# Linear attention and a mixture of adapters on one core: numerators one slot ahead, q three slots ahead, gating a step later

## The chip, the cores and the metric

The kernel runs on one core of one Trainium2 chip. The metric is the device time of one execution in microseconds (us). The engines are TensorE (PE, with the loads of its weights as PEld), VectorE (DVE), ScalarE (ACT), GpSimd (POOL) and SyncE (SP). Each has its own queue and they meet through semaphores. L257 is line 257 of the kernel before.

## The reference

Inputs are q, k and v of 8 batches, 8 heads, 576 positions and 64 features in fp32, and the weights of 8 adapters of rank 16. Cut to what matters:

```python
def phi(x):                     # c, s: cos and sin of pi/2 * position / 576
    r = np.maximum(x, 0.0)
    return np.concatenate([r * c, r * s], axis=-1)
q_p, k_p = phi(q), phi(k)                            # 128 features
kv = np.einsum('bhsf,bhsd->bhfd', k_p, v)            # per batch and head
z = np.sum(k_p, axis=2)
x = (q_p @ kv) / (q_p @ z + 1e-06)                   # heads side by side: 4608 x 512
logits = x @ w_gate                                  # 8 experts, the best two are taken
w = softmax over the two
out = x + sum over the two of w * ((x @ A[e]) @ B[e])
```

## The kernel before, in words

A batch has 576 = 9 x 64 positions; position 9 r + s is row r of block s. Two blocks make a *slot* of 128 tokens, so 8 batches make NT = 36 slots; slots 4, 13, 22 and 31 hold block 8 of two batches (`mixed`). The first slots that need kv of batch 1 to 7 are 4, 9, 13, 18, 22, 27 and 31.

The whole program order is written out by hand (`manual_schedule`): what a step emits stands in each engine's queue in just this order. The main loop runs over steps n = 0 to 34, and what the steps do is put together from these pieces:

- **k.** `load_k`, `load_q`, `load_v` are DMAs that POOL issues and that turn fp32 into bf16. A block of k is scaled by cos and by sin with its relu, as two instructions on ACT, on DVE (`scale_k1`, L151 and L153) or on POOL (L156); POOL's need the relu before them, `relu_k` on DVE (L165). `kv` (L180) multiplies a scaled block by v into the PSUM tiles `cd`; after the ninth block of a batch `kv_out` copies them on ACT (L188). The tables `kv_at`, `relu_at`, `pool_at`, `act_at` and `dve_at` say in which step each row stands; `first` is the batch's first slot, `at` the step in which its relus stand and its POOL rows start. When POOL's rows of batch b are issued, the loads of k and v of batch b + 3 and of q of batch b + 2 follow in its queue.
- **q.** `move_q(n)` turns the q of slot n with 16 (from slot 27 on 32 smaller) matmuls by diagonal matrices into two PSUM tiles of the pool `qd` (L213, L201), which has two buffers, and two copies with relu on ACT put it into `qpT` (L229).
- **Numerators.** `numden(n)` (L257) multiplies `qpT` by kv into `nd`, the 8 heads' numerators and denominators. `nd` has one buffer. Epsilon is added by a small matmul (L252), or, in steps after 13 that have rows of `kv`, by DVE (`eps_dve`).
- **Normalise.** `normalise(n)` on DVE: the reciprocal (L270) and the product (L277), giving `xt`, the slot's x.
- **Transposition.** `transp_x(n)` (L285) turns `xt` with four matmuls into the PSUM tile `xz`, of which there is one, and `evac_x` copies it on DVE (L291).
- **Logits and gate.** `logits(n)` (L311) gives gate logits and x A for all experts of a slot into `za` (one buffer for a group of three slots). Per group: `gate_a` on DVE (L320 to L328), `gate_sig` on ACT (L337), `gate_b` on DVE (L344, L346), then `transp_z` (L359) into the rest of `xz`, which the next `evac_x` takes along.
- **Output.** `emit(d)` is two matmuls, x by the identity and the gated part by B (L377, L382), a copy on ACT (L408) and the store by SP; later slots take the second matmul alone and add x on POOL (`delta_add`, L397, L402). In steps with rows of `kv` the output takes a buffer of `qd`, otherwise `cd`.

Step n stands in this order: `evac_x(n-1)`, `normalise(n)`, `move_q(n+1)`, rows of `kv`, early logits, gates, outputs, the sigmoid, `transp_x(n)`, `transp_z`, rows and relus of k, late logits, `numden(n+1)`, rows of k on ACT.

The stores are held back until k of the last batch has landed (`first_loads`). After the loop the last groups are gated and put out one by one.

Of the kernel before, what the change touches and what calls it, by code (L numbers as in the profile page):

```python
# [13 lines left out]
NS = 9  # L14
# [5 lines left out]
def kernel(ctx, tc, q, k, v, w_gate, A, Bw, out):  # L20
# [12 lines left out]

    persist = ctx.enter_context(tc.tile_pool(name="persist", bufs=1))
    p_kp = ctx.enter_context(tc.tile_pool(name="p_kp", bufs=3))
    p_qpt = ctx.enter_context(tc.tile_pool(name="p_qpt", bufs=6))
    p_kv = ctx.enter_context(tc.tile_pool(name="p_kv", bufs=3))
    p_x = ctx.enter_context(tc.tile_pool(name="p_x", bufs=14))
    p_xt = ctx.enter_context(tc.tile_pool(name="p_xt", bufs=7))
# [24 lines left out]
    def load_k(b, eng=None):  # L64
        load(eng or nc.gpsimd, k_b[b].rearrange("p g s d -> p g (s d)"), k, b)

    def load_q(b):
        load(nc.gpsimd, q_b[b].rearrange("p g s d -> p g (s d)"), q, b)

    def load_v(b):  # L70
        load(nc.gpsimd, v_b[b][:, 0:VN].rearrange("p (g x) -> p g x", g=G), v, b)
# [161 lines left out]
    def move_q(n):  # L233
        transp_q(n)
        evac_q(n, 0)
        evac_q(n, 1)
# [5 lines left out]
    def numden(n):  # L242
        nd_t[n] = nd = ps.tile([128, 2, 512], FP32, name="nd")
        tok = tokens(n)
        if mixed(n):
            jobs = [(lo, tok[0][0]), (hi, tok[1][0])]
        else:
            jobs = [(slice(0, 128), tok[0][0])]
        for gg in range(2):
            qpT = qpT_t.pop((n, gg))  # L250
            if not eps_dve(n):
                nc.tensor.matmul(out=nd[:, gg, D:4 * W:W], lhsT=ones, rhs=eps_hi, start=True,  # L252
                                 stop=False, skip_group_check=True)
            for j in range(4):
                h = 2 * j + gg if quad(n) else gg * 4 + j
                for pr, b in jobs:
                    nc.tensor.matmul(out=nd[pr, gg, j * W:(j + 1) * W],  # L257
                                     lhsT=qpT[:, j, pr], rhs=kv_t[b][:, h % 2, h // 2, :],
                                     start=(eps_dve(n) and j == 0), stop=(j == 3),
                                     skip_group_check=True)  # L260
# [21 lines left out]
    def transp_x(n):  # L282
        x = xt_t[n].rearrange("p (k c) -> p c k", c=DCH)
        for c in range(DCH):
            nc.tensor.transpose(out=xz[:, c * 128:(c + 1) * 128], in_=x[:, c], identity=ident)  # L285
# [140 lines left out]
    def put(at, step, what):  # L426
        at.setdefault(step, []).append(what)
# [5 lines left out]
    kv_at[3] = [(1, s) for s in (5, 4, 7, 8, 6)]  # L433
    for b in range(2, B):
        first = b // 2 * NS + b % 2 * 4
        at = {2: 5, 3: 8, 4: 12, 5: 17, 6: 20, 7: 23}[b]
        n_pool = {2: 5, 3: 7, 4: 8, 5: 8}.get(b, 9)
        for s0, s1 in ((0, 3), (3, n_pool)):
            put(relu_at, at, (b, s0, s1))
        for s in range(n_pool):  # L440
            put(pool_at, at, (b, s))
        for i in range(2):
            if n_pool <= 7:
                put(dve_at, at, (b, 7, i))
            if n_pool < 9:
                put(act_at, first - 4 + i, (b, 8, i))
            if n_pool == 5:
                put(act_at, first - 3 + i, (b, 6, i))
                put(act_at, first - 2, (b, 5, i))
        order = (7, 0, 1, 2, 3, 4, 8, 6, 5) if n_pool <= 7 else (0, 1, 2, 3, 4, 5, 8, 6, 7)  # L450
        if n_pool == 9:
            order = range(NS)
        for j, s in enumerate(order):

            if b == 2:
                ahead = 2 if j < 4 else 1
            elif b == 3:
                ahead = 3 if j < 2 else 2 if j < 5 else 1
            else:
                ahead = 4 - min(j // 2, 3)  # L460
            put(kv_at, first - ahead, (b, s))

    early_at, late_at, gate_a_at, gate_b_at, move_at = {}, {}, {}, {}, {}
    prev = 5
    for g, t in enumerate(groups[:-2]):
        at = max(t[-1] + 1, prev + 1)
        for n in t:
            if t[-1] + 1 < at or (n < t[-1] and prev == at - 1):  # L470
                put(late_at, at - 1, n)
            else:
                put(early_at, max(n + 1, at - 1), n)
        prev = at + 1
        put(gate_a_at, at, g)
        put(gate_b_at, at + 1, g)
        put(move_at, at + 2, g)
    put(late_at, NT - 2, NT - 3)

    with tc.manual_schedule():  # L480
# [17 lines left out]
        load_q(2)  # L498
        load_k(3)
        load_v(3)  # L500
        load_k(4)
        load_q(3)
        load_v(4)
        kv_out(0)
        transp_q(0)
        evac_q(0, 0, "dve")
        evac_q(0, 1)
        numden(0)

        g10, g11, g12 = range(len(groups) - 3, len(groups))  # L510
        todo, held = [], []
# [11 lines left out]
                held.append(d)  # L523

        for n in range(NT - 1):
            if n > 0:
                g = move_at.get(n - 1, (None,))[0]
                evac_x(n - 1, g)
                if g is not None:
                    todo += groups[g]  # L530
            normalise(n)
            if n != 3:
                move_q(n + 1)
            for b, s in kv_at.get(n, ()):
                kv(b, s)
                if kv_n[b] == NS:
                    kv_out(b)
            for t in early_at.get(n, ()):
                logits(t)
            if n == 3:  # L540
                move_q(n + 1)
            for g in gate_a_at.get(n, ()):
                gate_a(g)
            for g in gate_b_at.get(n, ()):
                gate_b(g)
            now = todo[:2 if len(todo) > 3 and n not in kv_at else 1]
            del todo[:len(now)]
            for d in now:
                emit(d, n not in kv_at, add=n > 27)
            for g in gate_a_at.get(n, ()):  # L550
                gate_sig(g)
            transp_x(n)
            for g in move_at.get(n, ()):
                transp_z(g)
            for b, s, i in dve_at.get(n, ()):
                scale_k1(b, s, i, "dve")
            for b, s0, s1 in relu_at.get(n, ()):
                relu_k(b, s0, s1)
            for b, s in pool_at.get(n, ()):
                scale_k(b, s)  # L560
                if (b, s) == pool_at[n][-1]:
                    if b + 3 < B:
                        load_k(b + 3)
                    if b + 2 < B:
                        load_q(b + 2)
                    if b + 3 < B:
                        load_v(b + 3)
                    if b + 3 == B - 1:

                        nc.sync.dma_start(out=first_loads, in_=k_b[B - 1][0:1, 0, 0, 0:8])  # L570
                        for d in held:
                            store(d)
                        held = None
            for t in late_at.get(n, ()):
                logits(t)
            numden(n + 1)
            for b, s, i in act_at.get(n, ()):
                scale_k1(b, s, i, "act")

# [56 lines left out]
```

## Time and profile before

| | before |
|---|---|
| time, median of 3 runs | 114.4 us (114.37 to 114.47) |
| the profiled execution: time | 114.54 us |
| its span | 112.8 us |
| PE busy, share of the span | 96.1 us, 85% |
| DVE | 83.7 us, 74% |
| ACT | 78.2 us, 69% |
| POOL | 72.3 us, 64% |

The profile is of one execution. "Busy" is the time in which an engine runs instructions; a group's row says how many instructions of one line there are, their busy time and mean, the engine's idle time just before them and what ended it. In a timeline a row gives the start, the length, the engine, the line and the tiles; equal neighbours are merged, and on PE the length reaches a little into the next row, since matmuls are pipelined.

### The profile page before, as it was taken

What the parts mean: (1) busy time and instruction counts of PE and PEld (TensorE: products, weight loads), DVE (VectorE), ACT (ScalarE), POOL (GpSimd) and SP (SyncE); (2) the same over time, 40 slices, a digit from 0 to 9 for tenths busy, and PEclk for the clock granted to TensorE, in tenths of its full rate; (3) what the DMA queues carried; (4) which work ended last, traced back from release to release, by engine and by line L of the source; (5) the groups of instructions that cost most, each with busy time, mean ns of one, the idle gap of its engine ahead of it and who ended that gap; (6) DMA issues with size and microseconds to landing.
All of it is one profiled execution on the core that took longest, in us unless ns stands there. A gap on an engine that the chain in (4) does not pass through costs nothing.

```text
span 112.8 us, 4956 instructions
## 1 busy us (share of the span) xinstructions
PE 96.1 (85%) x2050; PEld 74.1 (66%) x2068; DVE 83.7 (74%) x296; ACT 78.2 (69%) x169; POOL 72.3 (64%) x134
## 2 busy tenths in 40 slices
PE   2999676978899899999999999998998997978710
PEld 1347465867796788868788888785786886754200
DVE  5598489459969677695987998999949589786620
ACT  5087579755986595797876978856777777895720
POOL 5992223228995996299939999989980445774000
PEclk9999999999999999999999999999999999999998
DMA  2999999999999999999999999999999424526892
GB/s 41 385 206 208 213 202 210 210 180 208 208 208 209 207 209 209 209 206 213 204 207 208 208 209 208 242 348 383 381 324 366 142 100 97 185 101 226 285 340 82
DMA packets 19670, 24.77 MB, mean 220 GB/s; under 512 B 2624, under 2 KB 14528, under 8 KB 19648
## 3 DMA queue, kind: packets, MB, share of 16 engines
q0 software_dynamic: 13856, 13.84, 73.8%
q1 hardware_dynamic: 5792, 10.62, 26.9%
q8 instruction: 16, 0.26, 0.9%
q14 instruction: 6, 0.05, 0.1%
HBM read 28.85 MB, written 9.44 MB: 340 GB/s over the span
## 4 chain that ended last, share of the span: by engine, by line
PE 40%; DMA 28%; DVE 15%; issue 4%; POOL 4%; ACT 4%; POOLq 0%; DVEq 0%; ACTq 0%
DMA k<-in_k_dram 14%; DMA v<-in_v_dram 12%; PE cd L180 9%; PE za L311 7%; PE qd L213 6%; PE xz L285 5%; PE nd L257 4%; DVE xt L277 4%; PE dx L377 3%; DVE k L165 3%; DVE xT L291 2%; DVE zg L346 2%; ACT osb L408 2%; PE qd L201 2%; DMA out_dram<-osb 2%
## 5 line engine op out<-in xcount | busy, mean ns | idle before, releaser
L229 ACT ACTIVATE qpT<-qd 128x512 bf16<-128x512 f32 x71 | 38.6, 595 | 15.0 <-PE qd L213 10.9
L156 POOL TENSOR_SCALAR kp<-k,cos_tab 128x256 bf16<-128x256 bf16 x46 | 22.6, 490 | 7.1 <-DVE k L165 6.5
L277 DVE TENSOR_TENSOR xt<-nd,rden 128x512 bf16<-128x512 f32 x36 | 24.9, 691 | 1.3
L291 DVE COPY xT<-xz 128x512 bf16<-128x512 bf16 (+1 forms) x36 | 17.1, 476 | 9.9 <-PE xz L359 6.4
L156 POOL TENSOR_SCALAR kp<-k,sin_tab 128x256 bf16<-128x256 bf16 x46 | 21.9, 476 | 0.0
L180 PE MATMUL cd<-v,kp 64*128 64x128 bf16 x576 | 20.3, 217 | 0.9 <-DVE kp L153 0.9
L285 PEld LDWEIGHTS <-xt 128*128 128x128 bf16 x144 | 10.8, 115 | 12.1 <-DVE xt L277 7.9
L285 PE MATMUL xz<-ident,xt 128*128 128x128 bf16 x144 | 14.4, 222 | 5.0 <-DVE xt L277 4.3
L180 PEld LDWEIGHTS <-kp 64*128 64x128 bf16 x576 | 16.3, 94 | 3.1 <-issue 0.9
L257 PE MATMUL nd<-kvsb,qpT 128*128 128x65 bf16 (+1 forms) x320 | 16.7, 195 | 1.1 <-DVE qpT L231 0.5
L213 PE MATMUL qd<-diag,q 128*64 128x128 bf16 x432 | 17.3, 222 | 0.3 <-DMA q<-in_q_dram 0.3
L402 POOL TENSOR_TENSOR osb<-osb,xt 128x512 f32<-128x512 f32 x8 | 9.2, 1160 | 9.6 <-ACT osb L408 8.0
L408 ACT COPY osb<-dx 128x512 f32<-128x512 f32 x19 | 11.2, 588 | 5.9 <-remote 2.1
L213 PEld LDWEIGHTS <-q 128*64 128x64 bf16 x432 | 13.1, 109 | 1.8 <-DMA q<-in_q_dram 0.5
L257 PEld LDWEIGHTS <-qpT 128*128 128x128 bf16 (+1 forms) x320 | 12.7, 100 | 1.9 <-ACT qpT L229 0.7
L311 PE MATMUL za<-AW,xT 128*128 128x144 bf16 x140 | 12.4, 227 | 0.7 <-DVE zg L346 0.5
L311 PEld LDWEIGHTS <-xT 128*128 128x128 bf16 x144 | 9.0, 98 | 3.2 <-DVE xT L291 1.0
L408 ACT COPY osb<-cd 128x512 f32<-128x512 f32 x16 | 9.1, 597 | 1.3 <-PE cd L382 1.3
L62 POOL DMA_DIRECT2D v<-in_v_dram x8 | 6.2, 778 | 5.2 <-DMA q<-in_q_dram 4.4
L485 PE MATMUL wu<-wide,ones 128*128 128x512 bf16 x24 | 7.3, 477 | 2.0 <-DVE AW L115 2.0
L62 POOL DMA_DIRECT2D q<-in_q_dram x8 | 6.1, 763 | 3.6 <-DMA k<-in_k_dram 3.6
L62 POOL DMA_DIRECT2D k<-in_k_dram x7 | 5.4, 771 | 3.9 <-DMA k<-in_k_dram 2.2
(75 smaller groups left out, 133.8 us busy)
## 6 DMA issues: line engine op xcount, KB each, us to landing
out_dram<-osb SPq DMA_DIRECT2D x32, 256.0 KB, 3.9
v<-in_v_dram POOLq DMA_DIRECT2D x8, 576.0 KB, 16.5
q<-in_q_dram POOLq DMA_DIRECT2D x8, 576.0 KB, 15.6
k<-in_k_dram POOLq DMA_DIRECT2D x7, 576.0 KB, 15.5
k0f<-in_k_dram SPq DMA_DIRECT2D x1, 1152.0 KB, 5.4
out_dram<-osb SPq DMA_DIRECT2D x8, 128.0 KB, 2.4
AW<-in_moe_A_dram POOLq DMA_DIRECT2D x1, 128.0 KB, 18.2
Ball<-in_moe_B_dram POOLq DMA_DIRECT2D x1, 128.0 KB, 16.7
```

What stands on the lines that cost most here:

```text
L62: eng.dma_start(out=t, in_=rows(dram, b))
L156: nc.gpsimd.tensor_scalar(out=dst, in0=src, scalar1=tab, scalar2=1.0, op0=ALU.mult, op1=ALU.mult)
L180: nc.tensor.matmul(out=kvz[par][:, g], lhsT=kp_t[b][pr, s, g], rhs=v_rhs(b, g, s, pr), start=(first and g == 0), stop=(last and g == G - 1))
L213: nc.tensor.matmul(out=t[cols, j, 2 * gi:2 * gi + 2, :], lhsT=q_b[b][:, 2 * gp + gi, s, :], rhs=diag[:, s, i], start=(j == 0 and gi == 0), ...
L229: nc.scalar.activation(t, src, AF.Relu)
L257: nc.tensor.matmul(out=nd[pr, gg, j * W:(j + 1) * W], lhsT=qpT[:, j, pr], rhs=kv_t[b][:, h % 2, h // 2, :], start=(eps_dve(n) and j == 0), ...
L277: nc.vector.tensor_tensor(out=x, in0=nd[:, :, :, 0:D], in1=rden.rearrange("p (g j) -> p g j", g=2).to_broadcast([128, 2, 4, D]), op=ALU.mult)
L285: nc.tensor.transpose(out=xz[:, c * 128:(c + 1) * 128], in_=x[:, c], identity=ident)
L291: nc.vector.tensor_copy(t[:, 0:c], xz[:, 0:c * 128].rearrange("p (c s) -> p c s", c=c))
L311: nc.tensor.matmul(out=za_t[g][:, i, :], lhsT=xT[:, c, :], rhs=AW[:, :, c, :], start=(c == 0 and i == 0), stop=(c == DCH - 1), skip_group_ ...
L402: nc.gpsimd.tensor_tensor(out=t, in0=t, in1=xt_t.pop(n), op=ALU.add)
L408: nc.scalar.copy(t, src)
```

## The change

In a step n whose next slot is not in `late` (the first slots of the batches and the last three), `numden(n+1)` now stands right behind `normalise(n)`, ahead of `transp_x(n)`, and `transp_x` stands ahead of the rows of `kv`. `evac_x(n-1)` follows `normalise(n)` there. q is turned by a table: as a rule three slots ahead (`q_at`), for the second and third slot of batches 1, 2 and 3 behind the numerators of the first (`q_end`); `qpT` gets 8 buffers. A group's gate stands a step later, logits are put into other steps, and outputs follow. The relus and POOL rows of batches 2 to 7 start in steps 6, 10, 14, 17, 21 and 25 (before 5, 8, 12, 17, 20 and 23), some blocks go from POOL to ACT, and the rows of `kv` stand closer to the step that needs them. q of batch 3 is loaded ahead of k of batch 4.

```diff
@@ -33,7 +33,7 @@
     persist = ctx.enter_context(tc.tile_pool(name="persist", bufs=1))
     p_kp = ctx.enter_context(tc.tile_pool(name="p_kp", bufs=3))
-    p_qpt = ctx.enter_context(tc.tile_pool(name="p_qpt", bufs=6))
+    p_qpt = ctx.enter_context(tc.tile_pool(name="p_qpt", bufs=8))
     p_kv = ctx.enter_context(tc.tile_pool(name="p_kv", bufs=3))
     p_x = ctx.enter_context(tc.tile_pool(name="p_x", bufs=14))
     p_xt = ctx.enter_context(tc.tile_pool(name="p_xt", bufs=7))
@@ -433,8 +433,8 @@
     kv_at[3] = [(1, s) for s in (5, 4, 7, 8, 6)]
     for b in range(2, B):
         first = b // 2 * NS + b % 2 * 4
-        at = {2: 5, 3: 8, 4: 12, 5: 17, 6: 20, 7: 23}[b]
-        n_pool = {2: 5, 3: 7, 4: 8, 5: 8}.get(b, 9)
+        at = {2: 6, 3: 10, 4: 14, 5: 17, 6: 21, 7: 25}[b]
+        n_pool = {2: 5, 3: 6, 4: 8, 5: 8, 6: 8}.get(b, 9)
         for s0, s1 in ((0, 3), (3, n_pool)):
             put(relu_at, at, (b, s0, s1))
         for s in range(n_pool):
@@ -443,18 +443,19 @@
             if n_pool <= 7:
                 put(dve_at, at, (b, 7, i))
             if n_pool < 9:
-                put(act_at, first - 4 + i, (b, 8, i))
+                put(act_at, first - 3 if b < 4 else first - 4 + i, (b, 8, i))
+            if n_pool <= 6:
+                put(act_at, first - 2, (b, 6, i))
             if n_pool == 5:
-                put(act_at, first - 3 + i, (b, 6, i))
-                put(act_at, first - 2, (b, 5, i))
+                put(act_at, first - 3 + i, (b, 5, i))
         order = (7, 0, 1, 2, 3, 4, 8, 6, 5) if n_pool <= 7 else (0, 1, 2, 3, 4, 5, 8, 6, 7)
         if n_pool == 9:
             order = range(NS)
         for j, s in enumerate(order):
-            if b == 2:
+            if b < 4:
                 ahead = 2 if j < 4 else 1
-            elif b == 3:
+            elif b < 6:
                 ahead = 3 if j < 2 else 2 if j < 5 else 1
             else:
                 ahead = 4 - min(j // 2, 3)
@@ -462,15 +463,36 @@
+    firsts = [b // 2 * NS + b % 2 * 4 for b in range(B)]
+    late = firsts[1:] + [NT - 3, NT - 2, NT - 1]
+    q_at, q_end = {}, {}
+    for m in range(2, NT):
+        first = max(f for f in firsts if f <= m)
+        if first > 13:
+            put(q_at, m - 3, m)
+        elif first == 0:
+            put(q_at, m - 2, m)
+        elif m == first:
+            put(q_at, m - 1, m)
+        elif m <= first + 2:
+            put(q_end, first - 1, m)
+        else:
+            put(q_at, m - 3, m)
     early_at, late_at, gate_a_at, gate_b_at, move_at = {}, {}, {}, {}, {}
     prev = 5
     for g, t in enumerate(groups[:-2]):
-        at = max(t[-1] + 1, prev + 1)
+        at = max(t[-1] + 2, prev + 1)
+        if g == len(groups) - 3:
+            at = NT - 3
         for n in t:
-            if t[-1] + 1 < at or (n < t[-1] and prev == at - 1):
-                put(late_at, at - 1, n)
+            if n + 1 > prev:
+                put(early_at, n + 1, n)
             else:
-                put(early_at, max(n + 1, at - 1), n)
+                put(late_at, prev, n)
         prev = at + 1
         put(gate_a_at, at, g)
         put(gate_b_at, at + 1, g)
@@ -498,14 +520,15 @@
         load_q(2)
         load_k(3)
         load_v(3)
+        load_q(3)
         load_k(4)
-        load_q(3)
         load_v(4)
         kv_out(0)
         transp_q(0)
         evac_q(0, 0, "dve")
         evac_q(0, 1)
         numden(0)
+        move_q(1)
         g10, g11, g12 = range(len(groups) - 3, len(groups))
         todo, held = [], []
@@ -523,14 +546,28 @@
                 held.append(d)
         for n in range(NT - 1):
-            if n > 0:
+            def evac_before():
                 g = move_at.get(n - 1, (None,))[0]
                 evac_x(n - 1, g)
-                if g is not None:
-                    todo += groups[g]
+                return groups[g] if g is not None else []
+            if n > 0 and n in late:
+                todo += evac_before()
             normalise(n)
-            if n != 3:
-                move_q(n + 1)
+            if n + 1 not in late:
+                numden(n + 1)
+            if n > 0 and n not in late:
+                todo += evac_before()
+            for m in q_at.get(n, ()):
+                if m == n + 2:
+                    move_q(m)
+            if n + 1 not in late:
+                transp_x(n)
+                for g in move_at.get(n, ()):
+                    transp_z(g)
+            for m in q_at.get(n, ()):
+                if m != n + 2 and n != 3:
+                    move_q(m)
             for b, s in kv_at.get(n, ()):
                 kv(b, s)
                 if kv_n[b] == NS:
@@ -549,9 +586,10 @@
                 emit(d, n not in kv_at, add=n > 27)
             for g in gate_a_at.get(n, ()):
                 gate_sig(g)
-            transp_x(n)
-            for g in move_at.get(n, ()):
-                transp_z(g)
+            if n + 1 in late:
+                transp_x(n)
+                for g in move_at.get(n, ()):
+                    transp_z(g)
             for b, s, i in dve_at.get(n, ()):
                 scale_k1(b, s, i, "dve")
             for b, s0, s1 in relu_at.get(n, ()):
@@ -573,7 +611,10 @@
                         held = None
             for t in late_at.get(n, ()):
                 logits(t)
-            numden(n + 1)
+            if n + 1 in late:
+                numden(n + 1)
+            for m in q_end.get(n, ()):
+                move_q(m)
             for b, s, i in act_at.get(n, ()):
                 scale_k1(b, s, i, "act")
```

## The prediction

> **What bounds the kernel now.** I read the page's busy times first, then the groups with what ended the idle time before them, then the busy time by stretch, then the timelines of single steps.
>
> ```profile
> PE 96.1 (85%) x2050; PEld 74.1 (66%) x2068; DVE 83.7 (74%) x296; ACT 78.2 (69%) x169; POOL 72.3 (64%) x134
> L285 PE MATMUL xz<-ident,xt 128*128 128x128 bf16 x144 | 14.4, 222 | 5.0 <-DVE xt L277 4.3
> ```
>
> TensorE (PE) leads, and its one large idle group is the transposition of a slot (`transp_x`) waiting for VectorE's normalised slot `xt`. The next answer gives stretches: step 4 to 8, 9 to 12, 13 to 21, 22 to 30, 31 to 34 of the main loop. Columns: stretch, length, then busy time of PE, PEld, DVE, ACT, POOL, the granted clock, DMA share, GB/s.
>
> ```profile
> 23.50:34.80 11.30, 9.78 (x240) 8.61 (x236) 9.14 (x34) 8.29 (x19) 9.04 (x16) 1.00 1.28 207
> 34.80:47.90 13.10, 12.12 (x263) 10.01 (x265) 9.74 (x34) 8.74 (x21) 9.48 (x19) 1.00 1.21 208
> 47.90:70.50 22.60, 22.19 (x455) 17.94 (x463) 18.63 (x64) 18.02 (x39) 20.81 (x43) 1.00 1.21 208
> 70.50:93.30 22.80, 21.74 (x548) 17.63 (x547) 18.82 (x61) 16.62 (x35) 15.34 (x31) 1.00 0.87 285
> 93.30:101.70 8.40, 6.96 (x208) 5.46 (x212) 6.95 (x23) 6.87 (x16) 5.78 (x6) 1.00 0.38 122
> ```
>
> PE idles 1.5, 1.0, 0.4, 1.1 and 1.4 us: 5.4 in 78.2. Nothing that only reorders PE's work can win more than this here. So I count the waits of the new order on PE and compare them with 5.4.
>
> **The prices.** A plain step on PE (start times; the end column overlaps the next row, so the cost is the distance of the starts):
>
> ```profile
> 56.57 0.41 PE L257 MATMUL nd<-kvsb,qpT 128*128 128x65 bf16 x8
> 56.91 0.69 PE L213 MATMUL qd<-diag,q 128*64 128x128 bf16 x16
> 57.53 0.84 PE L180 MATMUL cd<-v,kp 64*128 64x128 bf16 x24
> 58.31 0.68 PE L311 MATMUL za<-AW,xT 128*128 128x144 bf16 x8
> 58.82 0.38 PE L377 MATMUL dx<-xt,ident 128*128 128x512 bf16 x1
> 59.25 0.39 PE L285 MATMUL xz<-ident,xt 128*128 128x128 bf16 x4
> 59.48 0.33 PE L359 MATMUL xz<-ident,zg 128*128 128x128 bf16 x3
> 59.64 0.41 PE L257 MATMUL nd<-kvsb,qpT 128*128 128x65 bf16 x8
> ```
>
> Numerators (`numden`) 0.34, turning q 0.62, one row of k into kv 0.78/3 = 0.26, logits of a slot 0.25, an output 0.43 (its second matmul's record is missing), `transp_x` 0.23, `transp_z` 0.16. VectorE:
>
> ```profile
> 25.32 0.20 DVE L270 RECIPROCAL rden<-nd 128x8 f32<-128x8 f32 x1
> ...
> 26.16 0.28 DVE L153 TENSOR_SCALAR kp<-k,cos_tab 128x256 bf16<-128x256 bf16 x1
> 26.55 0.70 DVE L165 TENSOR_SCALAR k<-k 128x768 bf16<-128x768 bf16 x2
> 27.18 0.41 DVE L291 COPY xT<-xz 128x512 bf16<-128x512 bf16 x1
> 28.64 0.31 DVE L320 MAX8 m<-za 128x8 f32<-128x8 f32 x3
> ...
> 29.28 0.41 DVE L291 COPY xT<-xz 128x512 bf16<-128x512 bf16 x1
> 30.53 0.17 DVE L344 TENSOR_TENSOR em<-za,mask 128x24 f32<-128x24 f32 x1
> 30.73 0.56 DVE L346 TENSOR_TENSOR zg<-za,em 128x384 bf16<-128x384 f32 x1
> ```
>
> `normalise` 0.84 to the next instruction (0.92 to its result), the row of k on DVE 0.39, the relu of k 0.63, `gate_a` 28.64 to 29.28 = 0.64, `gate_b` 0.75. PE, ACT and POOL around step 5:
>
> ```profile
> 23.33 0.61 PE L213 MATMUL qd<-diag,q 128*64 128x128 bf16 x16
> 25.19 0.64 PE L213 MATMUL qd<-diag,q 128*64 128x128 bf16 x16
> 26.30 0.41 PE L285 MATMUL xz<-ident,xt 128*128 128x128 bf16 x4 [0.47 <-DVE xt L277]
> 16.57 0.51 ACT L151 ACTIVATE kp<-k,cos_tab 128x256 bf16<-128x256 bf16 x1
> 23.82 1.08 ACT L229 ACTIVATE qpT<-qd 128x512 bf16<-128x512 f32 x2 [0.69 <-PE qd L213]
> 36.94 0.59 ACT L408 COPY osb<-cd 128x512 f32<-128x512 f32 x1
> 27.25 0.48 POOL L156 TENSOR_SCALAR kp<-k,cos_tab 128x256 bf16<-128x256 bf16 x1 [0.45 <-DVE k L165]
> 31.36 0.47 POOL L156 TENSOR_SCALAR kp<-k,sin_tab 128x256 bf16<-128x256 bf16 x1
> ```
>
> From PE free after the numerators (25.19) to the first instruction that needs their `xt` (26.30) are 1.11 us. `nd` has one buffer, so the next numerators wait for the same event. That is the change's rule: numerators n+1 may start 1.11 after numerators n if VectorE is free at once, and later by all that VectorE still has queued ahead of `normalise`.
>
> **Part by part.** All of it is order; PE's own work grows by 0.4: slots 14 and 18 lose the epsilon by DVE (four small matmuls on `ones`, 0.17 each in the row below, mostly overlapped: 0 to 0.7, I take 0.2), and one output adds `xt` on PE again (half an output, 0.21).
>
> ```profile
> L252 PE MATMUL nd<-eps_hi,ones 128*128 128x4 bf16 x40 | 6.5, 170 | 0.0
> 21.38 0.64 PE L213 MATMUL qd<-diag,q 128*64 128x128 bf16 x16
> 18.76 15.64 DMA k<-in_k_dram
> ```
>
> *Steps 0 to 3.* q of slot 3 is turned in step 1, so its two copies (1.08) now stand on ACT ahead of the scaled rows of k1, which began at 16.57. The new start is about 18.4, the rows are then ready some 0.4 apart, and kv 1 on PE ends up to 0.65 later than before, where the turning behind it started at 21.38. Bounds 0 and 0.65; I take 0.4.
>
> *Two turnings in a row (before slots 5/6, 10/11, 14/15).* `qd` has two buffers. The first turning starts at s; its copies run s+0.49 (23.33 to 23.82) to s+1.57; the second can end at about s+1.95 instead of s+1.24. Wait 0.7 each. It covers the 1.11 of the numerators, at this price. With 0.25 before numerators 6, whose `normalise` starts late, steps 4, 5 hold 1.0.
>
> *Step 6.* Set 0 at the end of logits 0 to 2. PE: numerators 7 and `transp_x`, done at 0.6, then numerators 8. VectorE's queue is gate_a 0, row 7 of k2, relu of k2, and only then `normalise` 7: 0.13 (numerators off PE at 25.19, `rden` at 25.32) + 0.64 + 0.39 + 0.63 + 0.92 = 2.7. PE waits 2.1. In the kernel before, the same k2 work stood a step earlier beside 0.75 of logits and ahead of no numerators. POOL starts the k2 rows after this relu: ten in 31.36 + 0.47 - 27.25 = 4.6; the third pair is 0.35 late for kv 2, and its copy on ACT holds numerators 9 another 0.3. Steps 4 to 8: 1.0 + 2.1 + 0.65 = 3.7.
>
> *Steps 9 to 12.* Two turnings 0.7. Step 10 repeats step 6: after logits 6 to 8 PE has numerators 11, transp_x, transp_z and an output, 1.2, and VectorE gate_a 2, row 7 of k3, relu, `normalise` 11, 2.7: wait 1.5. The twelve POOL instructions for k3 (5.5) make one row of kv 3 late by 0.3. Sum 2.5. The load of k3, which landed at 18.76 + 15.64 = 34.4, is no bound any more: step 10 comes at about 40.
>
> *Steps 13 to 17.* Two turnings 0.7. Step 13: from numerators 14 on, PE has transp_x, turn 16, outputs 4 and 5, numerators 15, transp_x, turn 17, output 6, two logits: 0.23 + 0.62 + 0.86 + 0.34 + 0.23 + 0.62 + 0.43 + 0.5 = 3.8. ACT: copies of q from 0.7 to 1.8, two outputs to 2.8, sigmoid to 3.0; VectorE: gate_b 3 to 3.75, the relu of k4 to 4.4, `normalise` 15 to 5.4. Numerators 16 wait 1.6. In step 17 turn 20 comes straight behind output 8, which holds a `qd` buffer for 0.2 + 0.59: wait 0.5. Sum 2.8.
>
> *Steps 18, 22, 27, 31.* Numerators of a batch's first slot still end their step (they need its kv), and numerators of the next slot now open the following step with nothing between. Four times 1.1 = 4.4, uncovered, straight from the row pair above.
>
> *Steps 19 to 30 else.* Step 26 repeats the `qd` wait, and numerators 25, 33 come near a late gate: 0 to 1.0; I take 0.5.
>
> *Steps 32 to 34.* q is turned already, so PE has little to cover: logits 30 wait for gate_b 9, whose sigmoid stands behind two copies of q and an output on ACT; `transp_x` 33 and 34 wait for `normalise` 0.6 to 1.0. 1.4 to 2.6; I take 2.0. The new extra output behind the loop stands beside ACT's idle time there.
>
> *The queues.* Loads k5, q4, v5 go out some 5 us later, k6 some 9; at 208 GB/s a load of 576 KB takes 2.8, and v4, four behind k3, lands near 46, so the stream first runs dry at k7, whose rows are needed long after. q3 ahead of k4 helps slot 13 and costs k4 2.8 of the 6 it has. Stores wait for k7 and start some 4 us later, with 30 us to drain. I price all this at nothing, and 3 us if this cover is gone.
>
> The relus of k are a gain or a loss too:
>
> ```profile
> 46.70 0.75 DVE L165 TENSOR_SCALAR k<-k 128x768 bf16<-128x768 bf16 x2
> 73.57 2.36 DVE L165 TENSOR_SCALAR k<-k 128x768 bf16<-128x768 bf16 x2
> ```
>
> The second ran while POOL scaled k6, the first with POOL idle. Moved to step 25, the relu of k7 finds POOL done by my order, a gain of 1.6 on DVE that lies beside PE's work. The Trainium skill, Advanced Engine Details and Errata, VectorE Performance Modes, says that VectorE's second SBUF port is shared with GpSimd and the two block each other; the two rows agree, and by it step 25 would cost 1.6 more if POOL were not done.
>
> **The sum.** 0.4 + 3.7 + 2.5 + 2.8 + 4.4 + 0.5 + 2.0 = 16.3 of waits, less the 5.4 of before, plus 0.4 of work = +11.3. The profiled execution has a span of 112.8 and a time of 114.5; so 124.1 and 125.8, and as the median of the runs is 0.1 under that execution, 125.7. Own range: 121 with the doubtful small terms at their low ends (0.4, three times 0.7, 0.65, 0.5, 0.5, 0.6 less), 127 with them at their high ends.
>
> **Rivals.** (a) *Only the uncoverable waits are real*: 4.4, 2.1, 1.5 and 1.6, the rest vanishing because slower PE lets ACT and POOL catch up: 9.6 - 5.4 + 0.4 = +4.6, 119.0. For: each of these has a queue or a single buffer behind it; against: the 0.7s hang on ACT's 1.08, which doesn't shrink. (b) *The stream of loads starves*: +3, 128.7 and up to 130.5. For: DMA runs at 208 GB/s without a gap until 70; against: the slack just worked out. (c) *The cover works, faster*: VectorE always reaches `normalise` n+1 before PE has done transp_x and the turn (0.85) and ACT keeps pace; then only the 4.4 are left, 4.4 - 5.4 + 0.4 = -0.6, 113.8. It decides at VectorE having under some 0.8 queued ahead of `normalise` in steps 6, 10 and 14; the rows above give 1.7, 1.7 and more. (d) *PE is not full*: PE's rows are spaced by waits inside them and close up once operands come early. PEld is busy 59.65 of the 78.2, so 13.1 could go: 125.7 - 13.1 = 112.6. Against: rows of the same kind keep their spacing with and without a wait before them (0.34 twice above). The Trainium skill, Perfetto Trace Analysis, Identifying the Most-Contended Engine, judges TensorE's headroom by LDWEIGHTS time and not by matmul time; it reads this trace as (d) does. (e) That the order isn't what the diff says, I exclude: it is written out by hand and each engine keeps it; its effect on the time would be none.
>
> **How the numbers follow.** Forecast 0.62, (a) 0.18, (b) 0.10, (c) 0.05, (d) 0.02, 0.03 left for no change where waits just balance 5.4. Range 118.5 to 130.5 takes in the forecast's own range, (a) and (b). Faster by over 0.2% (what this measurement can tell) 0.07, within 0.03, slower 0.90.
>
> **What would show it.** After: PE idle before `nd` of 1.1 in steps 18, 22, 27, 31, with DVE `xt` as releaser; of about 2 before numerators 8, 1.6 before 12 and 16, with gate, row and relu of k directly ahead of `rden` on DVE; `qd` waiting for ACT `qpT`. `normalise` 13 (47.9 now) at about 52, 31 (93.3 now) at about 104. It is wrong if PE's idle time between steps 4 and 34 stays under 8 us, or if DVE shows `rden` right behind `nd` in steps 6 and 10.

## The result and the profile after

| | before | after |
|---|---|---|
| time, median | 114.44 us (114.37 to 114.89) | 131.12 us (130.95 to 132.03) |
| span of the profiled execution | 112.8 us | 129.2 us |

The ratio is 1.1465, 95% interval 1.1403 to 1.1526. Slower, as forecast, but 131.1 lies above the range (118.5 to 130.5). For two kernels of the experiments (135.1 and 126.5 in their table) two of four executions were over 1.5% slower than the fastest; time and ratio are those of the faster two (the median of all four is 136.19 and 127.58), and the trace is of a slower one.

Page of the kernel after: busy times, the rows of the granted clock and of the load stream over 40 slices of 3.23 us, and three groups of PE.

```profile
PE 102.8 (80%) x2073; PEld 75.0 (58%) x2073; DVE 81.7 (63%) x294; ACT 79.8 (62%) x173; POOL 69.2 (54%) x129
...
PEclk9999999999999999999999999999999999599996
...
GB/s 67 355 207 208 208 208 207 188 207 209 207 207 210 209 206 213 205 210 205 34 2 154 211 211 302 264 381 385 294 139 41 86 86 126 36 167 106 291 296 121
...
L257 PE MATMUL nd<-kvsb,qpT 128*128 128x65 bf16 (+1 forms) x320 | 16.9, 196 | 5.9 <-DVE xt L277 4.6
...
L285 PE MATMUL xz<-ident,xt 128*128 128x128 bf16 x144 | 14.3, 223 | 1.0 <-DVE xt L277 0.9
...
L252 PE MATMUL nd<-eps_hi,ones 128*128 128x4 bf16 x44 | 7.4, 174 | 5.6 <-DVE xt L277 5.5
```

The change does what it says to the transposition: its idle time falls from 5.0 to 1.0 us. But the same releaser, VectorE's `xt`, now stands behind 10.1 us (4.6 + 5.5) of idle time ahead of the numerators and their epsilon. The wait was not removed; it was moved to an instruction with less work ahead of it.

The same five stretches as in the prediction (step 4 to 8, 9 to 12, 13 to 21, 22 to 30, 31 to 34), kernel after:

```profile
24.60:37.90 13.30, 10.03 (x242) 8.43 (x237) 8.54 (x32) 8.38 (x19) 8.46 (x16) 1.00 1.22 208
37.90:52.60 14.70, 12.38 (x259) 9.64 (x258) 8.77 (x28) 9.20 (x22) 8.34 (x16) 1.00 1.21 208
52.60:80.70 28.10, 24.74 (x506) 18.87 (x501) 18.55 (x63) 20.08 (x43) 20.81 (x43) 1.00 0.92 169
80.70:107.10 26.40, 22.58 (x582) 17.36 (x580) 17.78 (x63) 17.30 (x37) 15.16 (x31) 1.00 0.64 209
107.10:118.10 11.00, 7.68 (x147) 6.00 (x148) 7.76 (x29) 4.59 (x10) 5.66 (x5) 0.84 0.34 112
```

| steps | length before, after | forecast, measured | PE idle before, after | PE busy before, after |
|---|---|---|---|---|
| 4 to 8 | 11.30, 13.30 | +2.2, +2.0 | 1.5, 3.3 | 9.78, 10.03 |
| 9 to 12 | 13.10, 14.70 | +1.5, +1.6 | 1.0, 2.3 | 12.12, 12.38 |
| 13 to 21 | 22.60, 28.10 | +3.8, +5.5 | 0.4, 3.4 | 22.19, 24.74 |
| 22 to 30 | 22.80, 26.40 | +1.5, +3.6 | 1.1, 3.8 | 21.74, 22.58 |
| 31 to 34 | 8.40, 11.00 | +1.7, +2.6 | 1.4, 3.3 | 6.96, 7.68 |
| sum | 78.2, 93.5 | +10.7, +15.3 | 5.4, 16.1 | 72.8, 77.4 |

(The forecast column sorts the terms of the prediction's sum into these stretches, net of the idle time of before: of the 0.5 of steps 19 to 30, 0.1 is put to the third stretch and 0.4 to the fourth; the 0.4 of steps 0 to 3 and the 0.2 of the output behind the loop stand outside.) Idle time rose by 10.7, forecast 10.5. PE's busy time rose by 4.6 where the prediction had 0.2 in these steps. That is most of the miss; another 1.1 us, forecast 0.4, fell in steps 0 to 3, 0.4 of it ahead of slot 0 (`normalise` 0 at 13.85 instead of 13.42), where nothing differs.

PE's timeline after, the rows with waits:

```profile
25.58 0.90 PE L213 MATMUL qd<-diag,q 128*64 128x128 bf16 x16 [0.53 <-ACT qpT L229]
...
32.58 0.18 PE L252 MATMUL nd<-eps_hi,ones 128*128 128x4 bf16 x1 [2.01 <-DVE xt L277]
...
45.73 0.18 PE L252 MATMUL nd<-eps_hi,ones 128*128 128x4 bf16 x1 [1.48 <-DVE xt L277]
...
58.50 0.66 PE L311 MATMUL za<-AW,xT 128*128 128x144 bf16 x8 [0.35 <-DVE zg L346]
60.22 0.42 PE L257 MATMUL nd<-kvsb,qpT 128*128 128x65 bf16 x8 [1.05 <-DVE xt L277]
...
66.08 0.41 PE L213 MATMUL qd<-diag,q 128*64 128x128 bf16 x8 [0.33 <-ACT osb L408]
...
70.08 0.42 PE L257 MATMUL nd<-kvsb,qpT 128*128 128x65 bf16 x8 [1.03 <-DVE xt L277]
...
81.75 0.42 PE L257 MATMUL nd<-kvsb,qpT 128*128 128x65 bf16 x8 [1.03 <-DVE xt L277]
...
92.61 0.44 PE L201 MATMUL qd<-diag,q 64*64 64x64 bf16 x30 [0.53 <-ACT osb L408]
...
96.58 0.43 PE L257 MATMUL nd<-kvsb,qpT 128*128 128x65 bf16 x8 [1.22 <-DVE xt L277]
...
108.08 0.18 PE L252 MATMUL nd<-eps_hi,ones 128*128 128x4 bf16 x1 [1.03 <-DVE xt L277]
```

The large waits that the prediction named are there; the 0.3 each ahead of the rows of kv 3 and of numerators 9 are not. VectorE's timeline ahead of numerators 8 shows why the first is 2.0:

```profile
30.73 0.28 DVE L153 TENSOR_SCALAR kp<-k,cos_tab 128x256 bf16<-128x256 bf16 x1
30.92 0.28 DVE L153 TENSOR_SCALAR kp<-k,sin_tab 128x256 bf16<-128x256 bf16 x1
31.12 0.55 DVE L165 TENSOR_SCALAR k<-k 128x768 bf16<-128x768 bf16 x2
31.59 0.20 DVE L270 RECIPROCAL rden<-nd 128x8 f32<-128x8 f32 x1
```

Row and relu of k stand ahead of the reciprocal, which starts the moment they end.

### The profile page after: what moved, and what is told of

Its sections match the earlier page's. It is cut to its first block, busy times and chain, and to the rows that moved or that the text cites. A ratio compares the mean times of both kernels' runs of the same rounds, so it can differ in the third digit from the quotient of the medians.

```text
span 129.2 us, 4980 instructions
## 1 busy us (share of the span) xinstructions
PE 102.8 (80%) x2073; PEld 75.0 (58%) x2073; DVE 81.7 (63%) x294; ACT 79.8 (62%) x173; POOL 69.2 (54%) x129
## 4 chain that ended last, share of the span: by engine, by line
PE 54%; ACT 15%; DVE 14%; issue 5%; POOL 5%; DMA 3%; ACTq 0%
PE cd L180 11%; PE qd L213 8%; ACT qpT L229 8%; PE za L311 6%; PE wu L507 6%; PE nd L257 6%; DVE xt L277 4%; ACT osb L408 4%; POOL kp L156 4%; PE xz L285 4%; DMA out_dram<-osb 3%; PE dx L377 3%; PE qd L201 2%; PE dx L382 2%; DVE zg L346 2%
## 5 line engine op out<-in xcount | busy, mean ns | idle before, releaser
L156 POOL TENSOR_SCALAR kp<-k,cos_tab 128x256 bf16<-128x256 bf16 x44 | 21.2, 482 | 23.4 <-DVE k L165 22.3
L257 PE MATMUL nd<-kvsb,qpT 128*128 128x65 bf16 (+1 forms) x320 | 16.9, 196 | 5.9 <-DVE xt L277 4.6
L156 POOL TENSOR_SCALAR kp<-k,sin_tab 128x256 bf16<-128x256 bf16 x44 | 20.8, 473 | 0.0
L213 PE MATMUL qd<-diag,q 128*64 128x128 bf16 x432 | 18.1, 222 | 2.1 <-ACT qpT L229 1.6
L257 PEld LDWEIGHTS <-qpT 128*128 128x128 bf16 (+1 forms) x320 | 13.0, 100 | 9.3 <-DVE xt L277 4.9
L402 POOL TENSOR_TENSOR osb<-osb,xt 128x512 f32<-128x512 f32 x7 | 8.1, 1155 | 11.3 <-ACT osb L408 10.5
L408 ACT COPY osb<-cd 128x512 f32<-128x512 f32 x19 | 10.8, 594 | 4.1 <-PE cd L397 2.3
L408 ACT COPY osb<-dx 128x512 f32<-128x512 f32 x16 | 9.5, 593 | 5.1 <-PE dx L382 4.8
L311 PEld LDWEIGHTS <-xT 128*128 128x128 bf16 x144 | 10.0, 101 | 3.8 <-issue 0.8
L252 PE MATMUL nd<-eps_hi,ones 128*128 128x4 bf16 x44 | 7.4, 174 | 5.6 <-DVE xt L277 5.5
L507 PE MATMUL wu<-wide,ones 128*128 128x512 bf16 x24 | 8.1, 517 | 2.0 <-DVE AW L115 2.0
L270 DVE RECIPROCAL rden<-nd 128x8 f32<-128x8 f32 x22 | 4.5, 205 | 7.1 <-PE nd L257 7.1
```

What stands on the lines that cost most here:

```text
L156: nc.gpsimd.tensor_scalar(out=dst, in0=src, scalar1=tab, scalar2=1.0, op0=ALU.mult, op1=ALU.mult)
L213: nc.tensor.matmul(out=t[cols, j, 2 * gi:2 * gi + 2, :], lhsT=q_b[b][:, 2 * gp + gi, s, :], rhs=diag[:, s, i], start=(j == 0 and gi == 0), ...
L257: nc.tensor.matmul(out=nd[pr, gg, j * W:(j + 1) * W], lhsT=qpT[:, j, pr], rhs=kv_t[b][:, h % 2, h // 2, :], start=(eps_dve(n) and j == 0), ...
L311: nc.tensor.matmul(out=za_t[g][:, i, :], lhsT=xT[:, c, :], rhs=AW[:, :, c, :], start=(c == 0 and i == 0), stop=(c == DCH - 1), skip_group_ ...
L402: nc.gpsimd.tensor_tensor(out=t, in0=t, in1=xt_t.pop(n), op=ALU.add)
L408: nc.scalar.copy(t, src)
```

## The experiments

The kernels were made from one text, in which each part of the change can be taken or left, so their line numbers are one above those of the kernel after (L258 is L257). The theory: PE's queue is in order, and a numerator moved ahead waits out VectorE's round trip. The rivals: the loads (rows of k), or the ring of q alone, carry most of the price.

| numerators | gates | q ahead | rows of k | time, us | ratio, 95% | mean clock |
|---|---|---|---|---|---|---|
| old | old | one | new | 121.11 | 1.0579 (1.0526 to 1.0632) | 0.968 to 0.984 |
| old | new | one | old | 116.46 | 1.0179 (1.0164 to 1.0194) | 0.987 to 0.996 |
| old | old | three | old | 120.30 | 1.0517 (1.0497 to 1.0536) | 0.985 to 0.997 |
| new | old | three | old | 131.83 | 1.1533 (1.1509 to 1.1557) | 0.988 to 0.995 |
| new | new | three | old | 127.61 | 1.1123 (1.1025 to 1.1221) | 0.964 to 0.999 |
| new | old | three | new | 135.1 | 1.178 (1.171 to 1.185) | 0.978 to 0.979 |
| old | new | three | new | 132.16 | 1.1511 (1.1435 to 1.1587) | 0.939 to 0.966 |
| new | new | two | new | 127.23 | 1.1107 (1.1078 to 1.1137) | 0.986 to 0.999 |
| new | new | two | old | 126.5 | 1.1055 (1.0978 to 1.1133) | 0.967 to 0.980 |

The last column is the mean granted TensorE clock over each execution (0.972 to 0.999 for the kernel before, 0.950 to 0.986 for the kernel after). In some of them the clock is 0.50 for 3.41 us in the middle of work; one such period is some 0.013 of the mean, and what it costs is measured below, in the kernel with a turning behind more numerators. Eight buffers of `qpT` are in all these kernels, and q of batch 3 is loaded ahead of k of batch 4 wherever q is more than one slot ahead. The parts don't add up: rows, gates and q alone cost 6.7, 2.0 and 5.9, 14.6 together, and the numerators add 11.5 to q three ahead; that would be 26.1, and the whole is 16.7.

**Numerators undone.** All slots `late`, so that `transp_x` and `evac_x` stand where they were too; else as after.

```diff
-    late = firsts[1:] + [NT - 3, NT - 2, NT - 1]
+    late = list(range(NT + 1))
```

> The changed kernel with one part undone: every slot's numerators stand at the end of the step again, behind the transposition; q still three slots ahead, gates a step later, rows of k in their new places. Theory 'waits in queues' (PE stops wherever a result stands behind other work in an engine's queue): the four uncovered numerators (1.0 to 1.2 us each in the trace of after) go, and those of steps 6, 10, 14 lose a part: 123 to 126 us. Rival 'loads': the input stream runs dry at 61 to 68 us as in after, since POOL's rows of k and with them the loads stand where they stood: 130 to 131 us.

132.16, above both expectations: nothing is won back. So the numerators' waits are not a sum that goes away with them. A group of this kernel, then three stretches of 3.41 us in which the clock is 0.50, each behind the stretch before it (the last column but two is the clock):

```profile
L181 PE MATMUL cd<-v,kp 64*128 64x128 bf16 x576 | 21.6, 219 | 6.3 <-POOL kp L157 4.5 <-DMA v<-in_v_dram 0.7 <-issue 0.6
```

```profile
22.16:25.57 3.41, 2.17 (x55) 1.56 (x54) 1.32 (x3) 2.64 (x6) 1.07 (x3) 1.00 1.69 183
25.57:28.98 3.41, 3.38 (x49) 2.81 (x49) 1.32 (x3) 2.12 (x5) 1.21 (x2) 0.50 1.21 209
32.40:35.81 3.41, 1.39 (x32) 0.82 (x32) 2.12 (x7) 2.19 (x6) 3.08 (x7) 1.00 1.21 206
35.81:39.22 3.41, 3.41 (x48) 3.22 (x42) 1.15 (x3) 0.00 (x0) 3.41 (x7) 0.50 1.23 212
49.47:52.88 3.41, 1.59 (x29) 1.09 (x31) 1.76 (x5) 0.00 (x0) 3.41 (x9) 1.00 1.17 201
52.88:56.29 3.41, 3.41 (x54) 3.15 (x53) 1.32 (x3) 2.41 (x5) 3.41 (x7) 0.50 0.25 25
```

The rows of k into kv now wait 6.3 us (0.9 after), 4.5 of it for POOL. Whoever is not held up by the numerators is held up by the late rows. Behind stretches with much idle time the clock then falls, three times in this trace and once in that of the kernel after. That is not what hides a gain: at one mean clock, 0.966, one execution of each took 131.01 and 131.22 (after).

**Rows of k as before**, else as after.

```diff
-        at = {2: 6, 3: 10, 4: 14, 5: 17, 6: 21, 7: 25}[b]
-        n_pool = {2: 5, 3: 6, 4: 8, 5: 8, 6: 8}.get(b, 9)
+        at = {2: 5, 3: 8, 4: 12, 5: 17, 6: 20, 7: 23}[b]
+        n_pool = {2: 5, 3: 7, 4: 8, 5: 8}.get(b, 9)
...
```

> The changed kernel with the rows of k (relus, POOL's, DVE's, ACT's, kv) where they were before; numerators ahead, q ahead, gates later stay. 'Waits in queues': relus leave the queue in front of normalise in steps 6, 10, 14, the kv waits go, the uncovered four stay: 125 to 128 us. 'Loads': POOL issues loads as early as before, the stream no longer dries, and all that the change lost comes back but for its 0.4 us of work: 115 to 118 us.

127.61, in the range of the waits. The load stream of after stands nearly still in two slices (34 and 2 GB/s above, some 61 to 68 us); with the old rows it doesn't, and the rest stays slow. Starving loads are not the main price.

**Rows of k retimed alone**, on the kernel before.

```diff
-        at = {2: 5, 3: 8, 4: 12, 5: 17, 6: 20, 7: 23}[b]
+        at = {2: 6, 3: 10, 4: 14, 5: 17, 6: 21, 7: 25}[b]
...
```

> The kernel before with one part of the change: rows of k, relus, POOL's rows and kv in their new steps (6, 10, 14, 17, 21, 25). 'Waits in queues': POOL starts k2 and k3 one and two steps later, so kv 2 and 3 wait for their rows in steps 7, 8 and 11, 12 whatever the order of the numerators; in the run without the numerators ahead, normalise 13 came at 59.0 against 47.9 before: 119 to 124 us. 'The numerators are what costs': 114.5 to 116 us.

121.11, as the waits had it. PE's timeline and the group:

```profile
46.37 0.40 PE L181 MATMUL cd<-v,kp 64*128 64x128 bf16 x8 [0.59 <-POOL kp L157]
47.27 0.40 PE L181 MATMUL cd<-v,kp 64*128 64x128 bf16 x8 [0.51 <-POOL kp L157]
48.18 0.40 PE L181 MATMUL cd<-v,kp 64*128 64x128 bf16 x8 [0.51 <-POOL kp L157]
```

```profile
L181 PE MATMUL cd<-v,kp 64*128 64x128 bf16 x576 | 21.5, 217 | 3.9 <-POOL kp L157 3.6 <-DMA v<-in_v_dram 0.2 <-ACT kp L152 0.2
```

With relus one to two steps later, PE reaches the rows while POOL is still scaling, and goes at POOL's pace: a pair each 0.91 us (47.27 to 48.18). In the kernel after, PE is so late by then that only one such wait is left (0.42 at 34.48). These 3.9 us, at most 1.7 of half clock (34.13 to 37.54, PE busy throughout) and 1.0 ahead of slot 0 (`normalise` 0 at 14.46 instead of 13.42, where nothing differs) account for the span, 6.6 us longer than before.

**Gates as before**, else as after; and **gates later alone**, on the kernel before.

```diff
-        at = max(t[-1] + 1, prev + 1)
+        at = max(t[-1] + 2, prev + 1)
...
```

> The changed kernel with gates and outputs a step earlier, as before. 'Waits in queues': in the trace of after VectorE's gate_b waits 9.1 us in all for the sigmoid behind copies on ACT; with the gate a step earlier the order on ACT within a step is the same, so this falls little, while logits of the last slot of a group are now late beside the gate: 129 to 132 us. 'Loads': no change, 131 us.

> The kernel before with gates, logits and outputs a step later alone. 'Waits in queues': the gate is off every chain in the middle of the loop, only the last groups feel it: 114.5 to 116 us. 'The numerators are what costs': 114.5 us as well; above 117 us both would have missed a cost of the gate's place.

135.1, above both expectations, and 116.46, above the 116 of the waits. The gates of the first three groups and of the eleventh stand in the same steps by both rules; it is those of the fourth to the tenth that move. The later gate costs 2.0 alone and wins 4.0 once the numerators stand ahead: with the old gate the logits of step n stand on PE behind numerators n + 1, the maxima (`m`) on VectorE wait for these logits, and `normalise` n + 1 stands behind `m`. PE and VectorE then take turns instead of working side by side. Alone, 0.6 of its price stands ahead of slot 0 (`normalise` 0 at 14.00), 0.5 is a wait of kv 5 for POOL at 61.42, which had waited 4.17 for the relu behind the gate, and some 0.7 falls in the last steps.

**q three slots ahead alone; with the numerators too** (gates and rows as before). The first, on the kernel before:

```diff
-            if n != 3:
-                move_q(n + 1)
+            for m in q_at.get(n, ()):
...
+            for m in q_end.get(n, ()):
+                move_q(m)
```

The second adds to it:

```diff
+            if n + 1 not in late:
+                numden(n + 1)
```

> The kernel before with q turned three slots ahead alone (two turnings in a row before slots 5/6, 10/11, 14/15, q of slot 3 ahead of the rows of k1 on ACT). 'Waits in queues': 0.4 to 0.7 us at k1, 0.7 us at each of three double turnings, the last steps lose their cover: 116 to 118 us. 'The numerators are what costs': 114.5 to 115 us.

> The kernel before with numerators a slot ahead and q three slots ahead; gates and rows of k as before. 'Waits in queues': the four uncovered numerators 4.3 us, double turnings 2, k1 1, gates now ahead of normalise in VectorE's queue in more steps: 121 to 126 us. 'The numerators are what costs': nearly all of it, 128 to 132 us.

120.30, above all that I expected. PE and ScalarE in its step 9 to 10:

```profile
37.44 0.64 PE L214 MATMUL qd<-diag,q 128*64 128x128 bf16 x16
38.60 0.90 PE L214 MATMUL qd<-diag,q 128*64 128x128 bf16 x16 [0.53 <-ACT qpT L230]
39.76 0.90 PE L214 MATMUL qd<-diag,q 128*64 128x128 bf16 x16 [0.26 <-ACT qpT L230]
```

```profile
37.95 3.40 ACT L230 ACTIVATE qpT<-qd 128x512 bf16<-128x512 f32 x6 [0.80 <-PE qd L214]
```

Three turnings come at the pace of ScalarE's copies, 1.16 each (38.60 to 39.76) instead of 0.62, and `normalise` 9 to 10 takes 4.88 instead of 2.90. With `normalise` 4 to 5 (3.72 instead of 1.78) and 13 to 14 (4.34 instead of 2.04) that is 6.2 us, the whole price. Nor is this work paid back: from `normalise` 6 to 8, two steps without a turning, it takes 4.71 us instead of 4.85, and from 31 to 35, where slots are turned already, 8.23 instead of 8.43. Moving q's turning ahead moves PE work from where PE waits anyway to where it doesn't.

131.83 with the numerators, above the 121 to 126 of the waits and in the range of the rival, by which nearly all of the cost is theirs: they add 11.5 us here, with hardly a difference in clock. A wait of VectorE says how:

```profile
DVE m L321 <- PE za L312: 18.7, 9, 2.9
```

In the kernel before this wait is 1.5 us. It is the taking of turns described under the gates.

**A turning behind the numerators of slots 18, 22, 27, 31**, else as after.

```diff
+        elif first > 13 and m == first + 2:
+            put(q_end, first - 1, m)
```

> The changed kernel with the turning of q of slots 20, 24, 29 and 33 moved behind the numerators of slots 18, 22, 27 and 31, so that 0.57 us of work stand between these and the next numerators, which waited 1.03, 1.03, 1.22 and 1.03 us uncovered in after. 'Waits in queues': each wait falls by some 0.5, 2 us in all, 129 us. 'Loads': 131 us.

129.88 (1.1337, 1.1261 to 1.1414), 1.2 won of the 2.0. From `normalise` 18 to 19 it still takes 1.65: the turning fills the gap, and the gain comes where it stood. In the profiled executions 2.6 us are won behind `normalise` 9 (76.75 us from there to `normalise` 35 instead of 79.38), and 1.5 are lost just before it, in step 8, where both kernels have the same order. PE there, after, then with this edit, and this kernel's clock:

```profile
34.81 0.93 PE L311 MATMUL za<-AW,xT 128*128 128x144 bf16 x12
35.67 0.64 PE L213 MATMUL qd<-diag,q 128*64 128x128 bf16 x16
36.24 1.29 PE L180 MATMUL cd<-v,kp 64*128 64x128 bf16 x40
37.46 0.41 PE L285 MATMUL xz<-ident,xt 128*128 128x128 bf16 x4
```

```profile
34.60 1.62 PE L312 MATMUL za<-AW,xT 128*128 128x144 bf16 x12
36.15 1.06 PE L214 MATMUL qd<-diag,q 128*64 128x128 bf16 x16
37.15 1.58 PE L181 MATMUL cd<-v,kp 64*128 64x128 bf16 x40
38.66 0.41 PE L286 MATMUL xz<-ident,xt 128*128 128x128 bf16 x4
```

```profile
34.38:37.79 3.41, 3.41 (x50) 2.83 (x46) 0.73 (x7) 0.60 (x2) 3.41 (x7) 0.50 1.22 211
```

The same logits, turning and rows take 4.06 us instead of 2.65: one period of half clock cost 1.4 us where PE has work throughout. So most of the 2.0 is won, and the clock takes a part back.

**The last steps.** q of slot 32 behind numerators 31, slots 33 to 35 one step ahead, else as after.

```diff
+        elif m == 32:
+            put(q_end, 30, m)
+        elif m > 32:
+            put(q_at, m - 1, m)
```

> The changed kernel with the turnings of slots 32 to 35 back beside the steps that have little else: 32 behind the numerators of 31, 33, 34 and 35 one step ahead. In after the steps 31 to 34 take 11.0 us against 8.4 before, though PE has two turnings less in them, and the granted clock is 0.5 from 111.0 to 113.3. Theory 'nothing is refunded' (turnings pulled ahead cost their time in the middle, and the last steps, bound by chains through VectorE and ACT, don't get shorter): the wait behind numerators 31 is filled, PE keeps its clock, some 2 to 3 us less, 128 to 129 us. Rival 'the last steps are bound by the later gates alone': 131 us.

128.88 (1.1273, 1.1232 to 1.1314). `normalise` 31 comes at 106.11 (107.09 after) and 35 is 9.5 us later (11.0 after). After, then with this edit, in stretches around the logits of steps 32 and 33; the last column but two is the granted clock:

```profile
106.65:110.06 3.41, 1.95 (x62) 1.46 (x59) 3.11 (x12) 1.05 (x3) 1.15 (x1) 1.00 0.54 147
110.06:113.47 3.41, 3.14 (x57) 2.72 (x55) 1.17 (x3) 2.43 (x6) 1.89 (x2) 0.50 0.05 19
```

```profile
104.00:107.00 3.00, 2.45 (x80) 1.97 (x74) 1.84 (x6) 1.61 (x4) 1.84 (x2) 1.00 0.60 165
107.00:109.00 2.00, 1.71 (x48) 1.15 (x48) 1.58 (x10) 1.17 (x4) 0.00 (x0) 1.00 0.43 146
109.00:111.04 2.04, 1.52 (x35) 1.32 (x38) 1.28 (x4) 1.63 (x5) 1.49 (x2) 1.00 0.03 8
```

After, PE is busy 1.95 of 3.41 us, and then the clock is half; with q left to these steps it stays at 1.00. As expected; at most 1.6 of the 2.2 won is the clock's (PE busy 3.14 at 0.50).

**q two ahead, one turning behind each first slot's numerators**; then **with the rows of k as before too**.

```diff
+            if m == first:
+                put(q_at, m - 1, m)
+            elif m == first + 1 and first > 0:
+                put(q_end, first - 1, m)
+            else:
+                put(q_at, m - 2, m)
```

> The changed kernel with q turned two slots ahead everywhere: one turning, not two, stands behind the numerators of every first slot, also those of slots 18, 22, 27 and 31, which had none. 'Waits in queues and nothing refunded': no wait of the second turning for ACT's copies (0.53 and 0.3 us at three places), one turning less ahead at slot 18 (0.6), the four uncovered waits half filled (1.2 us in the run with the cover): 126 to 128 us. Rival 'the way ahead is needed': 131 us or more, since copies on ACT come just in time.

In the kernel before, q is turned one slot ahead. The second kernel has these turnings and, against the kernel after:

```diff
-        at = {2: 6, 3: 10, 4: 14, 5: 17, 6: 21, 7: 25}[b]
+        at = {2: 5, 3: 8, 4: 12, 5: 17, 6: 20, 7: 23}[b]
...
```

> Numerators one slot ahead and gates a step later as in the change, but q turned two slots ahead as before (one turning behind the numerators of every first slot), and the rows of k as before. If the rows' price is a wait on k that adds up with the rest (3.5 us in the changed kernel), 123 to 124.5 us. If the numerators ahead cost nothing by themselves once gates and turnings suit them, 114.5 to 117. If the rows of k only matter where q is three slots ahead, 127, as with the changed rows.

127.23 as expected, and 126.5, nearest to the third case: with this q the old rows win at most a little time (the intervals overlap). But the mean clock of the second is lower, 0.967 to 0.980 against 0.986 to 0.999, so what the old rows are worth at equal clock stays open. Numerators one slot ahead, later gates and q two slots ahead together cost 12 us over the kernel before; no run has q two ahead without the numerators, so their share isn't shown.

**A better kernel?** The first three groups' gates and logits placed by the rule of the change, on the kernel before:

```diff
+        if g < 3:
+            at = max(t[-1] + 2, prev + 1)
...
```

> The kernel before with the logits of the first three groups placed as in the change, the rest as before. With all gates later normalise 13 to 18 came 0.2 to 0.4 us earlier than before, and the loss of 2 us came behind slot 18 and in the last steps. If the gain is the logits' place: 114.1 us, 0.3 under before; if it was chance: 114.4 us.

114.38 against 114.42: 0.9983 (0.9968 to 0.9999). The edit moves nothing: for these groups both rules give logits in steps 5, 7 and 9 and gates in steps 6, 8 and 10, and VectorE, ScalarE and GpSimd run the same instructions in the same order as before. So this run says nothing of the gates; 0.2% is what two kernels of one order, with six and eight buffers of `qpT`, differ by. The gain of the kernel with all gates later (`normalise` 12 to 13 in 3.36 us instead of 3.77) stands in step 12, where the gate of the fourth group was; no run moves that one alone.

## Why the prediction was right and wrong

- **What bounds, and the 1.11.** Right. Idle time is where the limit lay: 16.1 us of PE idle in steps 4 to 34, forecast 15.9 (16.3 less the 0.4 of steps 0 to 3). By stretch it errs both ways: 3.3 for 3.7 in steps 4 to 8, 3.4 for 4.0 in 13 to 21, 3.8 for 2.6 in 22 to 30, where `qd` alone waits 0.53 at 92.61. That the sum fits so closely is luck in part. The four uncovered waits were 1.03, 1.03, 1.22 and 1.03 for 1.1.
- **Steps 6, 10, 13.** 2.01 and 1.48 for 2.1 and 1.5. Step 13's 1.6 came as 1.05 before numerators 16 and 0.35 before the logits ahead of them.
- **Two turnings in a row.** 0.53 ahead of each and 0.28 inside it (0.90 long instead of 0.62): 0.8 for 0.7. That this covers the numerators' 1.11 was right too: no wait stands before numerators 5, 10 and 14.
- **"All of it is order; PE's own work grows by 0.4".** Here it failed: PE's busy time grew by 4.6 in steps 4 to 34. 0.8 are the three stretched turnings, which the prediction had among the waits; 0.2 was forecast for the epsilon; at most 1.6 are the clock, below. The turnings that moved are no part of it: the same 31 stand in these steps before and after. Between `normalise` 13 and 18 turning takes 112 matmuls and 4.9 us instead of 80 and 3.3, two slots more; in steps 31 to 34 it takes 64 matmuls instead of 128, and PE waits there instead (idle 3.3 instead of 1.4, forecast 3.1). That q ahead has a price of its own is shown by the kernel with q alone (+5.9); the kernels with less of it agree (-3.9 with two ahead, -2.2 in the last steps alone), but in both the half clock of the last steps is gone too, and with two ahead the uncovered waits are half filled.
- **Steps 32 to 34, 2.0.** The waits had a term, the clock had none: it was left at 1.00, as in the rows of before. At 0.50 from 110.06 to 113.47, with PE busy 3.14, it costs at most 1.6 us of PE's time.
- **Steps 0 to 3, 0.4.** 1.1 measured, 0.4 of it ahead of slot 0; the rest wasn't followed.
- **Open.** Some 2 us of the longer busy time, or more, I can't assign. 0.4 of it may be in the logits: a pair of slots took 0.50 to 0.66 from start to start in front of numerators or a turning, where it took 0.51 in front of an output.
- **Rival (a), only the uncoverable waits,** 119.0: wrong, the small terms were real. **(b), the loads:** the stream ran dry, as (b) had it, but no wait on a load stands on PE after 35 us; its 3 us were 0. **(c), the cover works:** wrong, VectorE had 1.5 queued ahead of `normalise` 7 (30.08 to 31.59). **(d), PE is not full:** after, PEld is busy 58% of the span instead of 66%, and the span grew by 16 us: the room was there and was not won. The Trainium skill, Perfetto Trace Analysis, Identifying the Most-Contended Engine, reads headroom from LDWEIGHTS time; in this trace that headroom grew while the kernel got slower.
- **The relu of k7** took 0.83 (at 89.75, POOL idle) instead of the 2.36 that it took before, beside POOL's rows of k6, as forecast. The Trainium skill, Advanced Engine Details and Errata, VectorE Performance Modes, has the two engines share a port; the row agrees. It bought nothing, as forecast.
- **Signs.** `normalise` 13 at 52.59 (forecast 52), 31 at 107.09 (104): most of the miss of 3 lies between.

What was argued and not shown: that the numerators' own price is their waits on VectorE. Undoing them alone gave no time back, and waits for the late rows of k stood in their place; their price shows only in company, +11.5 over q three ahead.

## What to carry to other kernels

An in-order queue pays for a dependent instruction moved ahead with whatever stands in the other engine's queue: count that queue instruction by instruction, and the waits come out to 0.1 or 0.2 us. Work pulled ahead is not free because its sum is the same: it is paid at full price where the engine is full and repaid only if the place that it leaves was full too. And parts of a schedule that lean on each other can't be priced by undoing one: rows of k late, and numerators ahead, hide each other's waits. Before such kernels are compared, look at the clock of each: here idle time on PE was at times followed by half clock, and then paid twice.

## What the hardware showed that I had not expected

The granted TensorE clock fell to 0.50 in the middle of work, for 3.41 us at a time: once in the trace of the kernel after and in the traces of six of the twelve kernels of the experiments, not in that of the kernel before. PE's timeline of the kernel after:

```profile
111.80 1.17 PE L311 MATMUL za<-AW,xT 128*128 128x144 bf16 x8
```

The same eight logits took 0.66 at 58.50. Ahead of all 14 such periods PE had been busy for only 1.39 to 2.41 of the 3.41 us before; in the kernel with the turnings left to the last steps PE is busy 5.68 of 7.04 us and keeps 1.00. But the share of busy time alone doesn't decide. In the kernel with q alone PE is busy 1.89 of 3.41 us, and the clock stays:

```profile
27.86:31.27 3.41, 1.89 (x38) 1.71 (x36) 2.98 (x13) 1.42 (x3) 2.07 (x5) 1.00 1.21 209
31.27:34.68 3.41, 3.06 (x75) 2.65 (x74) 2.38 (x9) 2.21 (x6) 3.41 (x8) 1.00 1.21 208
```

What decides, these runs don't tell; that sparse work can make the work behind it slower is what a sum of waits leaves out.
